# Four staging buffers, an in-place filter product and moved steps in a fused FFT filter, SoLU and maxout kernel

## The chip, the cores and the metric

The kernel runs on one core of a Trainium2 chip. The metric is device time in microseconds (us), the median of three runs. The core has five engines that work side by side, each through its own list of instructions in order: TensorE (PE, matmuls), VectorE (DVE), ScalarE (ACT), GpSimd (POOL) and SyncE (SP, which here only starts DMAs). DMAs started on one engine's list form one queue.

## The reference, cut to what matters

```python
X = np.fft.rfft(x, axis=1)                      # x: (8, 3072, 256), float32
y = np.fft.irfft(X * (filt_r + 1j * filt_i), n=3072, axis=1)
t = y.reshape(8 * 3072, 256)
h = t @ w_in                                    # (256, 1024)
sm = exp(h - h.max(-1)) / (sum + 1e-9)
ln = layer_norm(h * sm) * g_ln                  # over 1024
t = ln @ w_out                                  # (1024, 256)
h = maximum(maximum(t @ w1, t @ w2), t @ w3)    # (256, 768) each
out = h @ w_out2                                # (768, 256)
```

The weights come as 64-bit floats and are turned into 32-bit ones on the chip.

## The kernel before, in words

Every matmul runs on pairs of 16-bit numbers, a high half and a low half of each 32-bit value, in three products. Results lie in PSUM, in a ring of six one-bank tiles (`rtile`, pool `ps_r`) and one two-bank tile for h.

**The FFT.** A sequence of 3072 is taken as 128 x 24. Step a (`a_item`, six pieces) transforms over 128 and stores to a scratch in DRAM (`scr_a`). Step b (`b_item`, u = 0 to 7) loads that back in another layout (`bin`), transforms over 24 and multiplies by the filter: VectorE forms two products p1 and p2 out of PSUM (lines 239, 240), GpSimd adds and subtracts their halves into `yf` (242, 243). Its `late` part splits `yf` into halves `yhl` (ACT 254, DVE 255; for batch 1 the second on GpSimd) and SP transposes them by DMA into `yt` (256). There are two `yhl` tiles, one for each half dc of the channels, used again by every u. Step c (`c_item`) goes back over 24, writes `zo`, transposes it by DMA (279) and stores it (`scr_z`, 291). Step d (`d_item`) loads `din` and goes back over 128. `prep_a` splits the input x for step a: ACT writes `xh` (147), DVE writes `xl` (152). `xh` and `zo` share one tag with two buffers, so an `xh` waits until the `zo` that had its buffer has been transposed away.

**The tiles.** 48 tiles of 512 tokens, six for each of the eight sequences (batches), each go through h (`h_item`, four pieces), z (two), m (six, three banks each: ACT 457 and DVE 459 evacuate, am) and o. The list `ORDER` (line 24; line 23 for the first tile) sets the order of these pieces by letters. The FFT steps of the next batches lie in five slots s0 to s4 of each tile, put there by the `put` calls (lines 702 to 751): for batches from 2 on, b for u = 0 to 7 in slots 0 and 2 of tiles 0 to 3, c for u = 7 in slot 1 of tile 4, and `prep_a` for the batch after that in the same slot behind it.

**The start.** Batch 0 has nothing to hide behind: x, filter and weights are loaded (x and filter on SP's queue, `w_in` on GpSimd's), then come six a pieces, ten rounds of b (round u) and c (round u, piece u-2) with weight work between (`steps`), then d and the first tile, with weight work between its h pieces (`fills`). `get(i)` loads a block of 512 KB of weights, `pre(i)` and `conv(...)` turn it into 32-bit floats (ACT 524, POOL 525; DVE 537, 539, 541).

`run(item)` calls an item's `early` part, then the `late` part that was held from the item before; `flush()` calls the held part at once. An m item's held part goes first.

Of the kernel before, what the change touches and what calls it, by code (L numbers as in the profile page):

```python
# [7 lines left out]
F32 = mybir.dt.float32  # L8
F16 = mybir.dt.float16
# [10 lines left out]
LEAST = 1.125 * 2.0 ** -15  # L20


FIRST = "s0 s1 h2 m0 x0 x1 m1 x0 s2 m2 x0 x0 x0 x0 x2 h3 m3 d m4 m5 g0 f o0 s3 o2 g1 s4"
ORDER = "z0 s0 z1 s1 h2 m0 x0 x0 x1 m1 x0 x0 s2 m2 x2 h3 m3 d m4 m5 g0 f o0 s3 o2 g1 s4"


@with_exitstack
def kernel(
# [41 lines left out]
    mhalf = cst.tile([128, 4], F32, name="mhalf")  # L70
    kap = cst.tile([128, 1], F32, name="kap")
    alpha_w = cst.tile([128, 1], F32, name="alpha_w")
    yhl_t = [cst.tile([128, 8, 128], F16, name=f"yhl{i}") for i in range(2)]

    scr_a = [drm.tile([128, 2, 24, 256], F16, name=f"scr_a{i}") for i in range(2)]
    scr_z = [drm.tile([6, 128, 2048], F16, name=f"scr_z{i}") for i in range(2)]
# [142 lines left out]
    def b_item(b, u):  # L219
        bi, bt, ft = bin_t.pop((b, u)), bt_t.pop((b, u)), f_t.pop((b, u))  # L220
        pss = []
        for dc in range(2):
            ps = rtile("bps")
            for k in range(8):
                o = ps[:, k * 48:(k + 1) * 48]
                xs = bi[:, k, dc * 128:dc * 128 + 128]
                PE.matmul(o, xs, bt[:, k, 0], start=True, stop=False)
                PE.matmul(o, xs, bt[:, k, 1], start=False, stop=True)
            pss.append(ps)
        yfs = []  # L230
        yt = two.tile([128, 2, 8, 128], F16, tag="yt", name="yt")
        yT_t[b, u] = yt

        def early():
            for dc in range(2):
                p1 = two.tile([128, 8, 2, 24], F32, tag="p1", name="p1")
                p2 = two.tile([128, 8, 2, 24], F32, tag="p2", name="p2")
                pv = pss[dc][:, :384].rearrange("p (k r s) -> p k r s", k=8, r=2)
                V.tensor_tensor(p1, pv, ft[:, dc, :, 0:1, :].to_broadcast([128, 8, 2, 24]), op=ALU.mult)
                V.tensor_tensor(p2, pv, ft[:, dc, :, 1:2, :].to_broadcast([128, 8, 2, 24]), op=ALU.mult)  # L240
                yf = two.tile([128, 8, 2, 24], F32, tag="yf", name="yf")
                G.tensor_tensor(yf[:, :, 0, :], p1[:, :, 0, :], p2[:, :, 1, :], op=ALU.subtract)
                G.tensor_tensor(yf[:, :, 1, :], p1[:, :, 1, :], p2[:, :, 0, :], op=ALU.add)
                if u == 0:

                    G.tensor_copy(yf[:, 0, 0, 0:1], p1[:, 0, 0, 0:1])
                    G.tensor_copy(yf[:, 0, 1, 0:1], p2[:, 0, 1, 0:1])
                yfs.append(yf)

        def late():  # L250
            for dc in range(2):
                yv = yfs[dc].rearrange("p k r s -> p k (r s)")
                yhl = yhl_t[dc]
                S.activation(yhl[:, :, 0:48], yv, AF.Copy)
# [447 lines left out]
    for b in range(1, NB):  # L702

        if b == 1:
            for i in range(6):
                put(0, 0, 3 if i < 2 else 4, absmax, 1, i)
            put(0, 0, 4, x_spread, 1)
            put(0, 1, 0, x_scale, 1)
            put(0, 1, 0, prep_a, 1, 0)
            put(0, 1, 0, prep_a, 1, 1)  # L710
            for s in range(6):
                put(0, 1, (1, 1, 2, 3, 3, 4)[s], do_a, 1, s)
            for u in range(2):
                put(0, 1, 2 * u, load_tabs, 1, u)
                put(0, 1, 4, load_b, 1, u)
            put(0, 1, 3, load_c, 1, 0)
        else:
            second = b == 2
            for i in range(6):
                at = ((2, 4), (2, 4), (3, 0), (3, 0), (3, 3), (3, 4)) if second else ((1, 0), (1, 2), (1, 4), (2, 1), (2, 2), (2, 4))  # L720
                put(b - 2, *at[i], absmax, b, i)
            put(b - 2, *((3, 4) if second else (3, 2)), x_spread, b)
            put(b - 2, 4, 0, x_scale, b)

            put(b - 2, 4, 1, prep_a, b, 0)
            put(b - 2, 4, 1, prep_a, b, 1)
            for s in range(6):
                put(b - 2, *((4, 3), (4, 4), (5, 0), (5, 0), (5, 1), (5, 2))[s], do_a, b, s)

            for u in range(2):  # L730
                put(b - 2, 4, 1 + 3 * u, load_tabs, b, u)
                put(b - 2, 5, 2, load_b, b, u)
            put(b - 2, 5, 0, load_c, b, 0)
# [25 lines left out]
    with tc.manual_schedule():  # L759
# [26 lines left out]
        tags = ["din", "din", "z", "ln0", "din", "din", "ln1", "ln2", "z", "ln3", "din", "din", "ln0", "ln1", "u", "u", "yt", "yt", "ao", "ao"]  # L786
        wln.append(two.tile([128, 2, 8, 512], F16, tag="ln", name="wln").rearrange("p a (i c) t -> p (a i) c t", i=2))
        got = {}

# [21 lines left out]
            return job  # L811

        for i in range(4):
            get(i, G)()
        prep_a(0, 0)
        prep_a(0, 1)
        for s in range(6):
            if s == 1:
                load_tabs(0, 0)
                load_tabs(0, 1)  # L820
            do_a(0, s)
            if s < 4:
                size_f(s)
        for s in range(4, 7):
# [9 lines left out]
        for u in range(2):  # L834
# [1 line left out]
        store_rest()  # L836
        load_c(0, 0)
        load_c(0, 1)
        get(6)()
        get(7)()  # L840
        scale_filter()
        scale_f(0, 0)
        scale_f(0, 1)
# [241 lines left out]
```

## Time and profile before

| | |
|---|---|
| median of three runs | 2996.73 us (2991.78 to 2999.52) |
| profiled execution | 2988.05 us, of which the span 2986.3 us |
| busy, share of the span | PE 93%, DVE 68%, ACT 42%, POOL 38% |
| DMA | 368 MB, 762734 packets |

The profile is of one execution, which ran 8.7 us below the median of the three. "Busy" is time in which an engine executed; "idle before" is the time just before an instruction in which its engine had none, with what ended it.

### The profile page before, as it was taken

Reading aid. Unit: us, or ns where it says so; the run is one execution under the profiler, and the core shown is the slowest. Engines: PE = TensorE matmul, PEld = TensorE weight load, DVE = VectorE, ACT = ScalarE, POOL = GpSimd, SP = SyncE. Lnnn points to the kernel's source line nnn. Section 1 sums busy time; section 2 is a strip of 40 time slices with the busy share of each in tenths; the row PEclk is TensorE's granted clock in tenths of the full one; section 3 lists DMA queues with packets and bytes.
Section 4 is the critical chain, followed back from the end, with each engine's and each line's share of the span. In section 5 each row is a group of like instructions: output and inputs, shape, how many; then the busy total and the mean of one; then the engine's idle time right before and its main releaser. Section 6 shows DMA issues by size and latency. Waiting matters only on the chain.

```text
span 2986.3 us, 49502 instructions
## 1 busy us (share of the span) xinstructions
PE 2791.1 (93%) x18992; PEld 1528.4 (51%) x18992; DVE 2016.4 (68%) x3971; ACT 1251.7 (42%) x2058; POOL 1147.5 (38%) x1187
## 2 busy tenths in 40 slices
PE   3478988999999999999999999999999999999999
PEld 1344544555545555455545555555554555555555
DVE  7787666667666776776767677667766767655653
ACT  4444433444344444444444444444444434433332
POOL 4433453245323443343433443234432444323222
PEclk7689999999999999999999999999999999999999
DMA  8924585468445765356733685447644456422221
GB/s 263 237 57 128 151 178 113 119 142 169 100 103 134 152 134 121 109 114 145 166 82 110 130 180 111 95 132 148 142 108 120 114 120 143 100 57 64 50 64 29
DMA packets 762734, 368.35 MB, mean 123 GB/s; under 512 B 650448, under 2 KB 707536, under 8 KB 762496
## 3 DMA queue, kind: packets, MB, share of 16 engines
q1 hardware_dynamic: 732992, 256.21, 39.6%
q0 software_dynamic: 29504, 108.98, 14.0%
q8 instruction: 149, 2.44, 0.4%
q14 instruction: 89, 0.73, 0.1%
HBM read 130.19 MB, written 75.50 MB: 69 GB/s over the span
## 4 chain that ended last, share of the span: by engine, by line
PE 44%; DVE 4%; DMA 3%; issue 2%; ACT 1%; POOL 1%; SPq 0%; ACTq 0%; DVEq 0%; POOLq 0%
PE mps L451 6%; PE mps L452 6%; PE mps L453 6%; PE hps L344 3%; PE hps L346 3%; PE hps L345 3%; PE zps L431 3%; PE zps L432 3%; PE zps L434 3%; PE ops L480 2%; PE ops L479 2%; PE ops L478 2%; DMA yt<-yhl 1%; DVE mx L355 1%; DMA zt<-zo 1%
## 5 line engine op out<-in xcount | busy, mean ns | idle before, releaser
L392 POOL TENSOR_TENSOR ul<-u,uh 128x1024 f16<-128x1024 f32 x191 | 406.5, 2128 | 1172.9 <-issue 627.0
L451 PE MATMUL mps<-z,wm 128*128 128x512 f16 x1728 | 660.2, 382 | 30.1 <-ACT am L457 22.9
L452 PE MATMUL mps<-z,wm 128*128 128x512 f16 x1728 | 659.9, 382 | 0.0
L453 PE MATMUL mps<-z,wm 128*128 128x512 f16 x1728 | 659.3, 382 | 0.0
L459 DVE SCALAR_TENSOR_TENSOR am<-mps,am 128x512 f32<-128x512 f32 x576 | 396.8, 689 | 210.5 <-ACT am L457 138.4
L355 DVE TENSOR_REDUCE mx<-hps 128x1 f32<-128x1024 f32 (+1 forms) x194 | 234.6, 1210 | 224.7 <-PE hps L346 224.4
L361 ACT ACTIVATE u<-hps,mx,scl 128x1024 f32<-128x1024 f32 (+1 forms) x194 | 232.1, 1196 | 357.0 <-DVE mx L358 350.6
L391 ACT ACTIVATE uh<-u 128x1024 f16<-128x1024 f32 x192 | 202.9, 1057 | 354.0 <-DVE u L372 353.9
L463 POOL TENSOR_TENSOR h<-am,h 128x512 f16<-128x512 f32 x240 | 278.4, 1160 | 149.6 <-ACT h L462 149.3
L478 PE MATMUL ops<-wo,h 128*128 128x256 f16 x1152 | 314.0, 273 | 4.2 <-ACT o L484 4.2
L462 ACT ACTIVATE h<-am 128x512 f16<-128x512 f32 x288 | 180.9, 628 | 317.7 <-DVE am L459 317.7
L480 PE MATMUL ops<-wo,h 128*128 128x256 f16 x1152 | 314.0, 273 | 0.0
L479 PE MATMUL ops<-wo,h 128*128 128x256 f16 x1152 | 314.0, 273 | 0.0
L372 DVE SCALAR_TENSOR_TENSOR u<-hps,mx,u 128x1024 f32<-128x1024 f32 (+1 forms) x194 | 246.7, 1273 | 99.0 <-ACT u L361 82.0
L344 PE MATMUL hps<-win,y 128*128 128x512 f16 x768 | 294.0, 383 | 10.8 <-DVE u L372 10.8
L346 PE MATMUL hps<-win,y 128*128 128x512 f16 x768 | 293.3, 382 | 0.8 <-DVE y L320 0.8
L345 PE MATMUL hps<-win,y 128*128 128x512 f16 x768 | 294.0, 383 | 0.0
L452 PEld LDWEIGHTS <-wm 128*128 128x128 f16 x1728 | 169.7, 98 | 233.4 <-issue 43.9
L431 PE MATMUL zps<-ln,wo 128*128 128x512 f16 x752 | 286.6, 381 | 1.8 <-ACT o L484 1.7
L432 PE MATMUL zps<-ln,wo 128*128 128x512 f16 x752 | 286.4, 381 | 0.0
L453 PEld LDWEIGHTS <-wm 128*128 128x128 f16 x1728 | 170.0, 98 | 207.7 <-issue 6.4
L451 PEld LDWEIGHTS <-wm 128*128 128x128 f16 x1728 | 169.9, 98 | 199.0 <-issue 6.2
(191 smaller groups left out, 4448.1 us busy)
## 6 DMA issues: line engine op xcount, KB each, us to landing
out_dram<-o SPq DMA_DIRECT2D x95, 256.0 KB, 2.3
scr_a<-ao SPq DMA_DIRECT2D x47, 512.0 KB, 3.2
scr_z<-zt SPq DMA_DIRECT2D x62, 384.0 KB, 4.4
din<-scr_z POOLq DMA_DIRECT2D x46, 512.0 KB, 5.3
xt<-in_x_dram POOLq DMA_DIRECT2D x42, 512.0 KB, 6.0
ft<-in_filt_dram POOLq DMA_DIRECT2D x56, 384.0 KB, 5.6
bin<-scr_a POOLq DMA_DIRECT2D x56, 384.0 KB, 6.2
bt<-in_dft_b_dram POOLq DMA_DIRECT2D x56, 144.0 KB, 4.0
```

Of the source, the lines that this page charges most:

```text
L344: PE.matmul(o, y[:, dc, 0, tk], win[:, 0, dc, w], start=(dc == 0), stop=False)
L345: PE.matmul(o, y[:, dc, 0, tk], win[:, 1, dc, w], start=False, stop=False)
L346: PE.matmul(o, y[:, dc, 1, tk], win[:, 0, dc, w], start=False, stop=(dc == 1))
L392: (V if (b, g, i) == (0, 0, 3) else G).tensor_tensor(ul, u, uh, op=ALU.subtract)
L431: PE.matmul(ps, wo1[:, 0, c, w], ln[:, 0, c], start=(c == 0), stop=False)
L432: PE.matmul(ps, wo1[:, 1, c, w], ln[:, 0, c], start=False, stop=False)
L451: PE.matmul(pss[k], wm[k][:, 0, dc, w], z[:, dc, 0], start=(dc == 0), stop=False)
L452: PE.matmul(pss[k], wm[k][:, 1, dc, w], z[:, dc, 0], start=False, stop=False)
L453: PE.matmul(pss[k], wm[k][:, 0, dc, w], z[:, dc, 1], start=False, stop=(dc == 1))
L459: V.scalar_tensor_tensor(am, ps, 2.0 ** -15, am, op0=ALU.mult, op1=ALU.max)
L478: PE.matmul(o, h2[:, j, 0, tk], wo2[:, 0, j], start=(j == 0), stop=False)
L479: PE.matmul(o, h2[:, j, 0, tk], wo2[:, 1, j], start=False, stop=False)
```

## The change

1. `yhl_t` has four tiles instead of two; u takes tiles 2 (u mod 2) + dc.
2. GpSimd writes the filter product back into p1 instead of into a tile `yf`. For u = 0 two values are kept in a small tile `mid` first and put back by one copy. So p1 is held until `yhl` has been made of it. In the start a `flush()` is put ahead of rounds 1 and 2.
3. `prep_a` of batches from 2 on goes from slot 1 to slot 2 of tile 4, and in `FIRST` and `ORDER` the whole slot 2 goes behind the third m piece (`s2 m2` becomes `m2 s2`).
4. The four loads of `w_in` go from GpSimd's queue to SP's, behind x and the filter. `get(6)` and `get(7)` go from behind the first c tables into the a pieces; `get(9)` from round 2 to round 0, `get(10)` and `get(11)` from round 4 to 3, `get(12)` and `get(13)` from round 5 to 8, `get(14)` and `get(15)` from round 6 to 9. Their `pre` and `conv` go along: blocks 12 to 15 are converted between the first h pieces instead of ahead of the first d.

```diff
-FIRST = "s0 s1 h2 m0 x0 x1 m1 x0 s2 m2 x0 x0 x0 x0 x2 h3 m3 d m4 m5 g0 f o0 s3 o2 g1 s4"
-ORDER = "z0 s0 z1 s1 h2 m0 x0 x0 x1 m1 x0 x0 s2 m2 x2 h3 m3 d m4 m5 g0 f o0 s3 o2 g1 s4"
+FIRST = "s0 s1 h2 m0 x0 x1 m1 x0 m2 s2 x0 x0 x0 x0 x2 h3 m3 d m4 m5 g0 f o0 s3 o2 g1 s4"
+ORDER = "z0 s0 z1 s1 h2 m0 x0 x0 x1 m1 x0 x0 m2 s2 x2 h3 m3 d m4 m5 g0 f o0 s3 o2 g1 s4"
...
-    yhl_t = [cst.tile([128, 8, 128], F16, name=f"yhl{i}") for i in range(2)]
+    yhl_t = [cst.tile([128, 8, 128], F16, name=f"yhl{i}") for i in range(4)]
...
-                yf = two.tile([128, 8, 2, 24], F32, tag="yf", name="yf")
-                G.tensor_tensor(yf[:, :, 0, :], p1[:, :, 0, :], p2[:, :, 1, :], op=ALU.subtract)
-                G.tensor_tensor(yf[:, :, 1, :], p1[:, :, 1, :], p2[:, :, 0, :], op=ALU.add)
...
+                    t = tiny.tile([128, 2], F32, tag="mid", name="mid")
+                    G.tensor_copy(t[:, 0:1], p1[:, 0, 0, 0:1])
+                    G.tensor_copy(t[:, 1:2], p2[:, 0, 1, 0:1])
+                G.tensor_tensor(p1[:, :, 0, :], p1[:, :, 0, :], p2[:, :, 1, :], op=ALU.subtract)
+                G.tensor_tensor(p1[:, :, 1, :], p1[:, :, 1, :], p2[:, :, 0, :], op=ALU.add)
+                if u == 0:
+                    G.tensor_copy(p1[:, 0, :, 0], t)
...
-            put(b - 2, 4, 1, prep_a, b, 0)
-            put(b - 2, 4, 1, prep_a, b, 1)
+            put(b - 2, 4, 2, prep_a, b, 0)
+            put(b - 2, 4, 2, prep_a, b, 1)
...
         for i in range(4):
-            get(i, G)()
+            get(i)()
...
+            if s in (1, 3):
+                get(6 + s // 2)()
...
+                if u in (1, 2):
+                    flush()
                 run(it)
...
-            [conv(0, 1), get(4), get(5)],
+            [conv(0, 1), get(4), get(5), get(9)],
...
-            [conv(4, 5), split(win[:, :, 0:1], win_32[0], "in"), pre(7)],
-            [split(win[:, :, 1:2], win_32[1], "in"), get(10), get(11), pre(8)],
-            [conv(6, 7), cen[0], pre(9), get(12), get(13)],
-            [cen[1], conv(8, 9), get(14), get(15), pre(10)],
+            [conv(4, 5), split(win[:, :, 0:1], win_32[0], "in"), pre(7), get(10), get(11)],
+            [split(win[:, :, 1:2], win_32[1], "in"), pre(8)],
+            [conv(6, 7), cen[0], pre(9)],
+            [cen[1], conv(8, 9), pre(10)],
...
+            [conv(10, 11), cen[3], cso[0], get(12), get(13)],
...
-            [cs[0][0], pre(16), pre(17)],
-            [conv(16, 17), cs[0][1], cs[1][0], pre(18), pre(19)],
-            [cs[1][1], cs[2][0]],
+            [conv(12, 13), cs[0][0], pre(14), pre(15)],
+            [conv(14, 15), cs[0][1], cs[1][0], pre(16), pre(17)],
+            [conv(16, 17), cs[1][1], cs[2][0], pre(18), pre(19)],
```

ScalarE's list in tile 4 of a batch, from the last c piece to the third h piece, before (`xh` is `prep_a`, `u` the exponentials of h, `am` the evacuation of m, `h_` its high half):

```order
L276 ACTIVATE zo<-cps 128x6x16x4 x2
L147 ACTIVATE xh<-xt,scl 128x1024 x2
L361 ACTIVATE u,st<-hps,mx,scl 128x1024
L457 ACTIVATE am<-mps 128x512
L391 ACTIVATE uh<-u 128x1024
```

and now:

```order
L278 ACTIVATE zo<-cps 128x6x16x4 x2
L363 ACTIVATE u,st<-hps,mx,scl 128x1024
L459 ACTIVATE am<-mps 128x512
L393 ACTIVATE uh<-u 128x1024
L464 ACTIVATE h_4835<-am 128x512
L459 ACTIVATE am<-mps 128x512
L464 ACTIVATE h_4835<-am 128x512
L459 ACTIVATE am<-mps 128x512
L147 ACTIVATE xh<-xt,scl 128x1024 x2
```

The two `xh` stood ahead of h's exponentials and the first m's evacuation; they stand behind the third m's.

VectorE's list in a tile with a b piece in slot 2, before (`p_` are the two products of each half, `am` two instructions for each m):

```order
L459 SCALAR_TENSOR_TENSOR am<-mps,am 128x512 x4
L239 TENSOR_TENSOR p_6099<-bps,ft 128x384
L240 TENSOR_TENSOR p_6100<-bps,ft 128x384
L239 TENSOR_TENSOR p_6106<-bps,ft 128x384
L240 TENSOR_TENSOR p_6107<-bps,ft 128x384
L459 SCALAR_TENSOR_TENSOR am<-mps,am 128x512 x2
L255 TENSOR_TENSOR yhl_88<-yf,yhl_88 128x8x48
L255 TENSOR_TENSOR yhl_89<-yf,yhl_89 128x8x48
L355 TENSOR_REDUCE mx<-hps 128x1
```

and now:

```order
L461 SCALAR_TENSOR_TENSOR am<-mps,am 128x512 x6
L239 TENSOR_TENSOR p_6106<-bps,ft 128x384
L240 TENSOR_TENSOR p_6107<-bps,ft 128x384
L239 TENSOR_TENSOR p_6112<-bps,ft 128x384
L240 TENSOR_TENSOR p_6113<-bps,ft 128x384
L357 TENSOR_REDUCE mx<-hps 128x1
```

The third m's two `am` stand ahead of the four products now, and the two `yhl`, which stood ahead of the fourth h piece's `mx`, stand behind that piece's `u`, ahead of the fourth m's `am`.

SP's list at the end of the c rounds, before (`zt` is the transposed `zo`):

```order
L279 DMA_TRANSPOSE zt<-zo 128x12x128 x2
L288 DMA scr_z_92<-zt 128x2x256 x2
L298 DMA din<-scr_z_92 128x2048 x2
L141 DMA scr_z_92<-zt 128x4x256 x2
L517 DMA wraw<-in_w_dram 128x2x512
```

and now:

```order
L281 DMA_TRANSPOSE zt<-zo 128x12x128
L519 DMA wln<-in_w_dram 128x2x512 x2
L281 DMA_TRANSPOSE zt<-zo 128x12x128
L519 DMA wln<-in_w_dram 128x2x512 x2
L290 DMA scr_z_94<-zt 128x2x256 x2
L300 DMA din<-scr_z_94 128x2048 x2
```

Four weight loads stand between the last transposes and the stores and loads of step d.

## Rows read from the trace of the kernel before

**Rows 1.** Page, part 1: busy time of the engines, share of the span, instructions.
```profile
PE 2791.1 (93%) x18992; PEld 1528.4 (51%) x18992; DVE 2016.4 (68%) x3971; ACT 1251.7 (42%) x2058; POOL 1147.5 (38%) x1187
```
**Rows 2.** Busy time by stretch: length, engines, granted clock, DMA share, GB/s.
```profile
46.00:126.00 80.00, 31.85 (x539) 26.75 (x540) 60.46 (x112) 37.26 (x67) 44.01 (x54) 0.54 1.09 260
138.20:171.70 33.50, 23.73 (x194) 15.41 (x195) 29.56 (x70) 17.01 (x28) 12.91 (x7) 0.89 0.36 103
500.00:2986.30 2486.30, 2441.09 (x16261) 1329.18 (x16259) 1667.68 (x3300) 1041.14 (x1724) 933.88 (x954) 1.00 0.51 115
```
**Rows 3.** PE's waits from 500 us on: releaser, us in total, times, longest.
```profile
PE mps L451 <- ACT am L457: 22.7, 7, 5.4
PE bps L227 <- DVE am L459: 6.0, 6, 1.2
PE aps L161 <- DVE am L459: 5.8, 6, 1.5
```
**Rows 4.** Busy time in five stretches of half clock: the first, and their sum.
```profile
846.40:852.20 5.80, 5.70 (x14) 2.08 (x14) 4.23 (x8) 2.22 (x4) 2.70 (x2) 0.50 0.20 45
...
sum 22.90, PE 18.85 PEld 6.76 DVE 18.71 ACT 10.56 POOL 4.19; mean PE 3.77 PEld 1.35 DVE 3.74 ACT 2.11 POOL 0.84
```
**Rows 5.** Instructions around 840 us: start, us, engine, what, idle before.
```profile
833.58 0.38 PE L451 MATMUL mps<-z,wm 128*128 128x512 f16 x1
840.70 1.15 ACT L147 ACTIVATE xh<-xt,scl 128x1024 f16<-128x1024 f32 x1 [7.68 <-DMA zt<-zo]
846.50 0.59 PE L451 MATMUL mps<-z,wm 128*128 128x512 f16 x1 [4.99 <-ACT am L457]
```
**Rows 6.** VectorE in a tile with b in slot 2, by time.
```profile
732.34 0.55 DVE L239 TENSOR_TENSOR p<-bps,ft 128x384 f32<-128x384 f32 x1
734.20 1.21 DVE L100 TENSOR_REDUCE xm<-xt 128x1 f32<-128x1024 f32 x1
736.72 1.08 DVE L255 TENSOR_TENSOR yhl<-yf,yhl 128x384 f16<-128x384 f32 x2
737.72 1.21 DVE L355 TENSOR_REDUCE mx<-hps 128x1 f32<-128x1024 f32 x1
742.89 1.48 DVE L459 SCALAR_TENSOR_TENSOR am<-mps,am 128x512 f32<-128x512 f32 x2
```
**Rows 7.** Instructions around 412 us, tile 3 of batch 0.
```profile
412.43 0.52 ACT L254 ACTIVATE yhl<-yf 128x384 f16<-128x384 f32 x1 [9.69 <-DMA yt<-yhl]
414.27 0.52 ACT L254 ACTIVATE yhl<-yf 128x384 f16<-128x384 f32 x1 [1.33 <-DMA yt<-yhl]
415.33 0.20 PE L268 MATMUL cps<-ct,yt 96*128 96x48 f16 x1 [9.75 <-ACT am L457]
```
**Rows 8.** VectorE's waits from 0 to 20 us.
```profile
DVE xm L100 <- DMA xt<-in_x_dram: 7.1, 5, 2.7
```
**Rows 9.** First matmul of c for u = 0, 3, 6, and of d.
```profile
61.77 0.22 PE L268 MATMUL cps<-ct,yt 96*128 96x48 f16 x1 [4.03 <-DMA yt<-yhl]
83.94 0.22 PE L268 MATMUL cps<-f,yt 96*128 96x48 f16 x1 [2.81 <-DMA yt<-yhl]
117.29 0.22 PE L268 MATMUL cps<-ct,yt 96*128 96x48 f16 x1 [6.80 <-DMA yt<-yhl]
134.51 0.29 PE L312 MATMUL dps<-dD,din 128*128 128x128 f16 x1 [8.06 <-DMA din<-scr_z]
```
**Rows 10.** ScalarE's waits from 46 to 126 us.
```profile
ACT yhl L254 <- DMA yt<-yhl: 19.7, 9, 5.8
```
**Rows 11.** Conversions on VectorE, and GpSimd beside one of them.
```profile
132.06 0.76 DVE L537 TENSOR_SCALAR wst<-wst 128x512 int32<-128x512 int32 x2
135.14 0.76 DVE L537 TENSOR_SCALAR wst<-wst 128x512 int32<-128x512 int32 x2
150.91 2.11 DVE L537 TENSOR_SCALAR wst<-wst 128x512 int32<-128x512 int32 x2
149.86 2.13 POOL L392 TENSOR_TENSOR ul<-u,uh 128x1024 f16<-128x1024 f32 x1 [0.63 <-ACT uh L391]
```

More of the change, by code (lines that the diff above doesn't have):

```diff
@@ L240, in early @@
                 V.tensor_tensor(p2, pv, ft[:, dc, :, 1:2, :].to_broadcast([128, 8, 2, 24]), op=ALU.mult)
-                yf = two.tile([128, 8, 2, 24], F32, tag="yf", name="yf")
-                G.tensor_tensor(yf[:, :, 0, :], p1[:, :, 0, :], p2[:, :, 1, :], op=ALU.subtract)
-                G.tensor_tensor(yf[:, :, 1, :], p1[:, :, 1, :], p2[:, :, 0, :], op=ALU.add)
                 if u == 0:
-                    G.tensor_copy(yf[:, 0, 0, 0:1], p1[:, 0, 0, 0:1])
-                    G.tensor_copy(yf[:, 0, 1, 0:1], p2[:, 0, 1, 0:1])
-                yfs.append(yf)
+                    t = tiny.tile([128, 2], F32, tag="mid", name="mid")
[5 more added lines that the diff above has]
+                    G.tensor_copy(p1[:, 0, :, 0], t)
+                yfs.append(p1)
         def late():
@@ L252, in late @@
                 yv = yfs[dc].rearrange("p k r s -> p k (r s)")
-                yhl = yhl_t[dc]
+                yhl = yhl_t[2 * (u % 2) + dc]
                 S.activation(yhl[:, :, 0:48], yv, AF.Copy)
@@ L785 @@
             todo += blocks(w_out, wo1_32[i], 4 * i)
-        tags = ["din", "din", "z", "ln0", "din", "din", "ln1", "ln2", "z", "ln3", "din", "din", "ln0", "ln1", "u", "u", "yt", "yt", "ao", "ao"]
+        tags = ["din", "din", "z", "ln0", "din", "din", "ln1", "ln2", "z", "ln3", "din", "din", "ln0", "ln1", "ln2", "ln3", "yt", "yt", "ao", "ao"]
         wln.append(two.tile([128, 2, 8, 512], F16, tag="ln", name="wln").rearrange("p a (i c) t -> p (a i) c t", i=2))
@@ L838 @@
         load_c(0, 1)
-        get(6)()
-        get(7)()
         scale_filter()
@@ L847 @@
         steps = [
-            [conv(0, 1), get(4), get(5)],
+            [conv(0, 1), get(4), get(5), get(9)],
             [conv(2, 3), csw[0], pre(4), pre(5), get(8)],
-            [csw[1], scale("in", 0, 2), pre(6), get(9)],
-            [conv(4, 5), split(win[:, :, 0:1], win_32[0], "in"), pre(7)],
-            [split(win[:, :, 1:2], win_32[1], "in"), get(10), get(11), pre(8)],
-            [conv(6, 7), cen[0], pre(9), get(12), get(13)],
-            [cen[1], conv(8, 9), get(14), get(15), pre(10)],
+            [csw[1], scale("in", 0, 2), pre(6)],
+            [conv(4, 5), split(win[:, :, 0:1], win_32[0], "in"), pre(7), get(10), get(11)],
+            [split(win[:, :, 1:2], win_32[1], "in"), pre(8)],
+            [conv(6, 7), cen[0], pre(9)],
+            [cen[1], conv(8, 9), pre(10)],
             [cen[2], pre(11)],
-            [conv(10, 11), cen[3], cso[0], pre(12), pre(13)],
-            [cso[1], scale("o1", 2, 1), pre(14), pre(15), split(wo1[:, :, 0:4], wo1_32[0], "o1"), split(wo1[:, :, 4:8], wo1_32[1], "o1")],
+            [conv(10, 11), cen[3], cso[0], get(12), get(13)],
+            [cso[1], scale("o1", 2, 1), get(14), get(15), split(wo1[:, :, 0:4], wo1_32[0], "o1"), split(wo1[:, :, 4:8], wo1_32[1], "o1")],
         ]
@@ L904 @@
             V.tensor_tensor(scl[0][:, k:k + 1], scl[0][:, k:k + 1], alpha_w, op=ALU.mult)
-        conv(12, 13)()
-        conv(14, 15)()
+        pre(12)()
+        pre(13)()
         run(d_item(0, 0))
```

## The prediction

> **What bounds the kernel now.** The page's first part comes first: TensorE is busy for 93% of the span, VectorE for 68% [rows 1]. Then the stretches: from 500 us to the end TensorE works 2441.1 of 2486.3 us, so it is the bound there, and what can be won is its 45 us without work and the little that runs at half clock; from 46 to 126 us it works 31.9 of 80 us, at a granted clock of 0.54, while the DMA engines' share is 1.09: the start is bound by transfers and the chain through them [rows 2]. Third, TensorE's waits from 500 us on: 22.7 us in 7 waits of a matmul of m for ScalarE's `am`, 6.0 us of b and 5.8 us of a for VectorE's `am`, six times each [rows 3]. The first of these is one event per batch, and its instructions tell the mechanism: an `xh` of `prep_a` sits on ScalarE with 7.68 us idle before it, until a transpose of `zo` has landed; h's exponentials and the first `am` queue behind it; TensorE, which has filled the six PSUM banks by 841.5, stands for 4.99 us [rows 5]. The same wait, 3.6 to 5.4 us long, comes in five batches; the other two of the 7 are under 0.4 us, so the five hold about 22 us. Towards its end the granted clock falls to half for 3 to 7 us; in those stretches TensorE worked 18.85 us, of which half, 9.4 us, is loss [rows 4].
>
> **The change part by part.** The sum is made against the profiled execution, 2988.05 us, which lies 8.7 us under the median 2996.73; I carry the difference over to the median.
>
> *`prep_a` in slot 2, slot 2 behind the third m.* The `xh` are issued some 11.9 us later: h, then three m of 18 matmuls at 7.93 us for 36 [rows 5]. The third m ends at about 833.6 + 11.9 = 845.5, the transpose had landed by 840.7 [rows 5]: 4.8 us to spare, so the wait should be gone and with it the idle time that precedes the fall of the clock. Gain 22 + 9.4, taken as 31. What is late next is VectorE, which now has the two `xl` between the third m and the fourth h. Before the fourth m's second bank is needed by the fifth m, TensorE has h (12 matmuls, 2.6 us), m (4.0), d (24 of a quarter width, 1.3) and two thirds of an m (2.6): 10.5 us. VectorE's chain in that time: the last `am` 0.7, two `xl` 2.5 (my estimate from the conversion of the same size, `mx`, at 1.21 each), h from `mx` to `am` 742.89 - 737.72 = 5.2, one `am` 0.7 [rows 6]: 9.1 us. It fits. Bounds: gain 20 (a third comes back) to 32.
>
> *b and a behind the third m.* 24 tiles of batches 2 to 7 and 2 of batch 1 have a b in slot 2. The banks that b waited for are free by then, so the 6.0 + 5.8 us [rows 3] go. In return VectorE's four products (734.20 - 732.34 = 1.9 us) and, behind h, the two `yhl` (1.0 us) stand ahead of the fourth m's `am`: 0.7 + 1.9 + 5.2 + 1.0 + 0.7 = 9.5 us against 10.5, and 10.6 in the ten tiles that also take a maximum of x (`xm`, 1.1) there [rows 6]. In the tile of rows 6 VectorE enters the stretch late, and I make it up to 2 us of waiting in about five such tiles, a few tenths in others: 8 to 12 us, against 11.8 saved. Taken as 0; bounds: 12 won to 15 lost.
>
> *Four `yhl`, batch 1.* At 412 us ScalarE stood 9.69 us for the old `yhl` buffer's transpose and held TensorE for 9.75 us [rows 7]. With other buffers the `yhl`, the two `am` behind it and the third m (moved ahead of c) go on: 4 us of work into the gap. c itself needs the very transposes that landed at 412.4 and 414.3 [rows 7], so it cannot start earlier than 412.4, and b comes at about 415; the third m, 4 us, and part of its half clock are saved behind it: taken as 7; bounds 3 to 9.
>
> *The start, x.* VectorE waited 7.1 us in 5 waits for x, 2.7 of them the first transfer's delay [rows 8]; `w_in` shared the DMA engines. Behind x it does not: 4.4 us of waits at most, taken as 3.7. `w_in` itself is first touched 20 us later.
>
> *The start, weight loads.* c went from u = 0 to 3 in 22.2 us and from 3 to 6, the rounds with two loads each, in 33.4 [rows 9]: 3.7 us more for each pair. Two pairs leave these rounds (7.5), two loads leave the time ahead of round 1 for the a pieces (0 to 3.7, taken as 2). But the two pairs stand ahead of the last stores and of `din` on the same queue now, where c's u = 6 to d took 17.2 us [rows 9]: between 0 and 7.5 come back, taken as 4. The trace shows the DMA share at 1.09 in all of that time [rows 2], so work moved inside it costs there what it cost before. The Trainium skill (DMA: Bandwidth & Descriptors, Queues, rings and completion order) says that on each DMA engine the descriptors of one issuing engine's ring are taken in ring order; by that all of the 7.5 us would return and the sum below would be 3.5 us smaller, and no run here shows it yet.
>
> *The start, four `yhl`.* ScalarE waited 19.7 us in 9 waits for the transposes of the round before [rows 10]. With the DMA engines full most of it will be waited elsewhere, by c for `yt`, as it was before each of the rows' c [rows 9]: bounds 0 and 10, taken as 3. The GpSimd work is the same but for one copy more at each u = 0 half; p1 is held longer, but VectorE makes `yhl` itself ahead of the next p1, so nothing new is waited for.
>
> *The start, conversions.* Blocks 12 to 15 were converted from 132.06 on, two pairs at 3.1 us (135.14 - 132.06) [rows 11], while `din` was on its way: d's result had to wait about 1.6 us for them. They go between the h pieces, where VectorE worked 29.6 of 33.5 us [rows 2]: 6.2 us more, less 1.6. Beside GpSimd the first step of a conversion took 2.11 us for two instead of 0.76: a subtraction of GpSimd ran from 149.86 to 151.99 [rows 11]. I take 6.4 us lost; bounds 3 and 9. The Trainium skill (SBUF — State Buffer, Who interferes with whom) has it that VectorE's faster two-port modes and GpSimd exclude each other for a whole instruction, the later one standing until the other ends; the two rows agree, and if every moved first step met a GpSimd instruction the loss would be 6.2 - 1.6 + 2 x 1.35 = 7.3 instead of 6.4.
>
> Start: 3.7 + 7.5 + 2 - 4 + 3 - 6.4 = 5.8 us won; bounds 14 won, 6 lost. All together: 31 + 0 + 7 + 5.8 = 44 us. 2988 - 44 = 2944 for a profiled execution, 2996.7 - 44 = **2953** for the median.
>
> **Rivals.**
> *Half of it.* The five waits go, but slot 2 costs its worse bound (15 lost) and start and batch 1 give nothing: 31 - 15 = 16 us, 2980. For it: the start is bound by DMA, where work is only moved. Against: x and batch 1 show waits that simply lose their cause.
> *The wait comes back.* The `xh` and `xl` stand ahead of the fourth h now; if the chain of 9.1 us is 4 us longer than I add up, the fifth m stands about as long as the third did, and the clock falls again. 44 - 31 = 13 us remain, and with a start that wins nothing 7 us: 2990, no change to tell. Against it: the spare 1.4 us, and ScalarE idle for 7.68 us before.
> *Slower.* The place is the fifth m in the 26 tiles with b in slot 2: VectorE's chain is 9.5 to 10.6 us against 10.5. `yhl` also waits for GpSimd's products, which stand behind the third m's `h`. The cost is 26 us for each microsecond over; it takes more than (44 + 9)/26 = 2.0 us over in each to be slower by over 9 us. At 2.3 us: 44 - 60, so 3013. For it: the chain is within a tenth of the window. Against: only part of the tiles carry the maximum, and VectorE is idle for a third of the span.
> *The ring order of the late loads* by itself moves d by 3.5 us and stays inside the range.
>
> **How the numbers follow.** A measurement of this kernel can tell about 0.3%, 9 us, from no change. Forecast 0.67, half of it 0.15, the wait comes back 0.10, slower 0.08. Faster: 0.67 + 0.15 + a little of the third = 0.83; the same 0.10; slower 0.07. The forecast's own range adds its bounds in part: 31 (20 to 32), slot 2 (15 lost to 12 won), batch 1 (3 to 9), start (6 lost to 14 won); all at their best 67 won, which gives 2930, at their worst 2 won. The range runs from 2930 to 2983, which takes in the second case and leaves the third and fourth out.
>
> **What would show it.** Right: no `xh` with some 7 us idle before it, no matmul of m waiting 3.6 us or more for `am` after 500 us, no half clock after 500 us; the gap of 9.75 us in batch 1 at 3 to 5; VectorE's waits for x at 3 us; d's first matmul between 120 and 130 us. Wrong: waits of m for VectorE's `am` of over 1 us in most tiles with b in slot 2, or d later than 134.5.

## The result, and the profile after

The changed kernel takes **2955.44 us** (median of four runs, 2949.55 to 2963.97) beside 2994.26 us before (2983.62 to 2999.52): ratio 0.9877, 95% interval 0.984 to 0.9914. The profiled execution took 2949.55 us, its span 2947.8, against 2988.05 before: 38.5 us less. Helper lines have moved by two: 451 is 453 now, 457 is 459, 459 is 461, 254 and 255 are 256 and 257, 268 is 270, 312 is 314, 355 is 357, 537 is 539.

Three instants cut the run into parts. The first `mx` of h on VectorE is the end of the FFT start; `amps`, a tiny product that scales the next batch's x, comes once per batch in the tiles, first for batch 1 and then for batch 2. The kernel before, timelines of DVE and PE (start, us, engine, line, operation, tiles, idle before):

```profile
141.33 1.22 DVE L355 TENSOR_REDUCE mx<-hps 128x1 f32<-128x1024 f32 x1 [1.83 <-PE hps L346]
258.32 0.80 PE L116 MATMUL amps<-dg,ones 128*128 128x128 f32 x2 [5.65 <-DVE dg L110]
466.46 0.76 PE L116 MATMUL amps<-dg,ones 128*128 128x128 f32 x2 [1.40 <-DVE dg L110]
```

The changed kernel, the same three rows:

```profile
141.40 1.22 DVE L357 TENSOR_REDUCE mx<-hps 128x1 f32<-128x1024 f32 x1 [1.90 <-PE hps L348]
268.52 0.80 PE L116 MATMUL amps<-dg,ones 128*128 128x128 f32 x2 [5.64 <-DVE dg L110]
467.37 0.77 PE L116 MATMUL amps<-dg,ones 128*128 128x128 f32 x2 [1.51 <-DVE dg L110]
```

So up to the first `mx` nothing is won (0.1 us later); from there to the first `amps` it takes 127.1 us instead of 117.0, **10.1 lost**; between the two `amps` 198.9 instead of 208.1, **9.2 won**; and from there to the end 2480.4 instead of 2519.8, **39.4 won**. The sum is the 38.5 us.

**The tiles.** The changed kernel by stretch (columns as in [rows 2]):

```profile
46.00:126.00 80.00, 31.77 (x539) 26.20 (x536) 62.02 (x116) 35.66 (x63) 42.34 (x54) 0.56 1.04 234
138.20:171.70 33.50, 19.22 (x110) 9.99 (x109) 29.65 (x59) 14.37 (x23) 11.54 (x7) 0.81 0.31 96
500.00:2947.80 2447.80, 2429.49 (x16251) 1325.34 (x16248) 1657.00 (x3299) 1033.41 (x1721) 933.27 (x961) 1.00 0.51 116
```

From 500 us on TensorE is without work for 2447.8 - 2429.5 = 18.3 us; it was 45.2 [rows 2]. Its waits there, changed kernel (releaser, us, times, longest):

```profile
PE mps L453 <- DVE am L461: 9.5, 13, 1.2
PE mps L453 <- ACT am L459: 2.9, 6, 0.5
PE bps L227 <- ACT o L486: 2.2, 1, 2.2
```

The 22.7 us for ScalarE's `am` and the 11.8 us of b and a [rows 3] are gone; m's waits for VectorE's `am`, 4.6 us in nine waits before, are 9.5 now, more than half of them in one tile per batch (below). The half clock after 500 us is one stretch (granted clock third from the end) where [rows 4] had five; it begins when the wait of 2.2 us for ScalarE's `o`, the third row above, ends (651.09):

```profile
651.30:654.70 3.40, 3.40 (x22) 1.44 (x19) 2.08 (x3) 2.81 (x6) 0.00 (x0) 0.50 0.20 77
```

The event of [rows 5], now ScalarE's timeline of the changed kernel in the same tile:

```profile
840.60 0.58 ACT L459 ACTIVATE am<-mps 128x512 f32<-128x512 f32 x1
842.73 0.63 ACT L464 ACTIVATE h<-am 128x512 f16<-128x512 f32 x1 [1.55 <-DVE am L461]
843.26 0.58 ACT L459 ACTIVATE am<-mps 128x512 f32<-128x512 f32 x1
843.74 2.17 ACT L147 ACTIVATE xh<-xt,scl 128x1024 f16<-128x1024 f32 x2
```

The two `xh` follow the third m's `am` without a gap; the 7.68 us in front of them are gone. VectorE's chain behind them held too, though the two `xl` took 3.37 us and not 2.5. The tight place is the tile of [rows 6], with its maximum of x. PE there, changed kernel:

```profile
740.98 0.38 PE L453 MATMUL mps<-z,wm 128*128 128x512 f16 x1 [0.53 <-ACT am L459]
743.61 0.38 PE L453 MATMUL mps<-z,wm 128*128 128x512 f16 x1 [1.17 <-DVE am L461]
```

0.53 + 1.17 = 1.7 us, once in each of five batches.

**Batch 1.** The tile of [rows 7], changed kernel, ScalarE and PE:

```profile
421.11 0.58 ACT L459 ACTIVATE am<-mps 128x512 f32<-128x512 f32 x1
423.01 0.20 PE L270 MATMUL cps<-ct,yt 96*128 96x48 f16 x1 [1.92 <-DMA yt<-yhl]
```

ScalarE evacuates m where it stood 9.69 us for a `yhl` buffer; c waits 1.92 us, not 9.75, and for its own transposes.

**The start.** VectorE's waits for x from 0 to 20 us, changed kernel ([rows 8] had 7.1 us):

```profile
DVE xm L100 <- DMA xt<-in_x_dram: 3.1, 3, 1.5
```

First matmuls of c for u = 0, 3 and 6, and of d, changed kernel (61.77, 83.94, 117.29 and 134.51 in [rows 9]):

```profile
63.96 0.22 PE L270 MATMUL cps<-ct,yt 96*128 96x48 f16 x1 [10.51 <-DMA yt<-yhl]
88.89 0.22 PE L270 MATMUL cps<-f,yt 96*128 96x48 f16 x1 [6.37 <-DMA yt<-yhl]
113.08 0.22 PE L270 MATMUL cps<-ct,yt 96*128 96x48 f16 x1 [5.44 <-DMA yt<-yhl]
135.40 0.29 PE L314 MATMUL dps<-dD,din 128*128 128x128 f16 x1 [12.72 <-DMA din<-scr_z]
```

VectorE waits 4.0 us less for x, and step a's scale, `amps` of batch 0, comes 2.7 us earlier (PE, before and now):

```profile
17.16 0.80 PE L116 MATMUL amps<-dg,ones 128*128 128x128 f32 x2 [17.16 <-DVE dg L110]
14.45 0.79 PE L116 MATMUL amps<-dg,ones 128*128 128x128 f32 x2 [14.45 <-DVE dg L110]
```

By c of u = 0 that is spent: c comes 2.2 us later, with three loads instead of two directly ahead of the first transposes. u = 6 comes 4.2 us earlier, and d, behind the four late loads, 0.9 us later. ScalarE's 19.7 us for the transposes [rows 10] have no row any more in 46 to 126 us, but c's waits for `yt` up to d sum to 34.8 us, against 35.7 before: the wait went elsewhere.

Then the conversions between the h pieces, DVE of the changed kernel:

```profile
145.50 0.75 DVE L539 TENSOR_SCALAR wst<-wst 128x512 int32<-128x512 int32 x2
146.16 1.70 DVE L541 SCALAR_TENSOR_TENSOR wst<-wln,wst 128x512 int32<-128x512 int32 x2
147.78 1.69 DVE L543 SCALAR_TENSOR_TENSOR wst<-wln,wst 128x512 int32<-128x512 int32 x2
149.40 0.68 DVE L357 TENSOR_REDUCE mx<-hps 128x1 f32<-128x512 f32 x1
```

VectorE has no gap here: the second piece's `mx` starts at 149.40, against 145.42 in the kernel before. That pair took 3.9 us. One pair stood ahead of the third piece already in the kernel before; the other new one, between the third and the fourth, took 3.8 us.

### The profile page after: what moved, and what is told of

It is laid out like the page before. It is cut to its first block, busy times and chain, and to the rows that moved or that the text cites. A ratio compares the mean times of both kernels' runs of the same rounds, so it can differ in the third digit from the quotient of the medians.

```text
span 2947.8 us, 49485 instructions
## 1 busy us (share of the span) xinstructions
PE 2780.9 (94%) x18992; PEld 1526.4 (52%) x18992; DVE 2010.1 (68%) x3973; ACT 1245.8 (42%) x2058; POOL 1151.0 (39%) x1199
## 4 chain that ended last, share of the span: by engine, by line
PE 58%; DVE 10%; issue 6%; POOL 3%; ACT 1%; DMA 1%; SPq 0%; DVEq 0%; ACTq 0%; POOLq 0%
PE mps L453 8%; PE mps L454 8%; PE mps L455 8%; PE zps L433 4%; PE zps L434 4%; PE zps L436 4%; PE hps L346 3%; PE hps L347 3%; PE hps L348 3%; PE ops L481 3%; PE ops L482 3%; PE ops L480 3%; DVE am L461 2%; POOL ul L394 1%; DVE mv L378 1%
## 5 line engine op out<-in xcount | busy, mean ns | idle before, releaser
L453 PE MATMUL mps<-z,wm 128*128 128x512 f16 x1728 | 655.7, 379 | 14.8 <-DVE am L461 11.5
```

The source lines that it names most:

```text
L453: PE.matmul(pss[k], wm[k][:, 0, dc, w], z[:, dc, 0], start=(dc == 0), stop=False)
```

## The experiments

Times are medians; ratios are to the kernel before on the same chip, with the 95% interval. The parts of every profile, as cut above (one execution each, us):

| kernel | first mx | mx to amps | amps to amps | to the end |
|---|---|---|---|---|
| before | 141.3 | 117.0 | 208.1 | 2519.8 |
| changed | 141.4 | 127.1 | 198.9 | 2480.4 |
| changed, again (g1) | 143.0 | 127.5 | 202.5 | 2483.3 |
| part 3 alone (e1) | 146.3 | 116.3 | 208.8 | 2485.8 |
| order alone (e2) | 145.4 | 116.3 | 209.4 | 2516.8 |
| prep_a alone (e3) | 145.7 | 116.0 | 208.5 | 2488.7 |
| part 4 undone (e4) | 143.7 | 116.2 | 201.8 | 2484.4 |
| two yhl (f1) | 143.3 | 127.3 | 210.1 | 2482.6 |
| late loads back (f2) | 140.2 | 127.3 | 203.1 | 2483.4 |
| and conversions back (f3) | 145.7 | 116.0 | 202.0 | 2478.8 |
| conversions in rounds (f4) | 144.3 | 118.0 | 202.4 | 2488.9 |
| four blocks less (g2) | 139.3 | 118.0 | 199.1 | 2493.9 |
| f3, w_in on GpSimd (g3) | 145.6 | 117.9 | 202.8 | 2487.9 |
| f3, block 9 later (g4) | 141.0 | 116.2 | 205.9 | 2487.1 |

What is the same code moves by up to 5 us in the first column (before, e1, e2 and e3 have one start), and by some 15 in the last; the second holds to 1 us in these four. A difference of a few us in the first and the last column tells nothing by itself.

**e1, part 3 alone**, on the kernel before:

```diff
-... x1 m1 x0 x0 s2 m2 x2 h3 ...
+... x1 m1 x0 x0 m2 s2 x2 h3 ...
-            put(b - 2, 4, 1, prep_a, b, 0)
+            put(b - 2, 4, 2, prep_a, b, 0)
```

> The kernel before with part 3 alone: slot 2 behind the third m and prep_a in slot 2; buffers, filter product and start as before. My theory (the steady state is won by the move of prep_a, which takes five waits of about 4.5 us and the half clock behind them; b behind the third m gives its 11.8 us of waits back): 31 to 42 us less than before, 2952 to 2963; no matmul of m waits over 3.6 us for am after 500 us, no half clock there but single short ones; the 9.75 us gap of batch 1 stays. Rival (the four yhl buffers and the in-place product are needed for the steady state): under 20 us less. Rival (the chain of VectorE in slot 2 costs): m waits for VectorE's am in most tiles with b, over 5 us in all.

2957.17 us, ratio 0.9869 (0.9848 to 0.9889). Most of the gain is in this part, without any new buffer. m's waits for VectorE's `am` are 11.5 us in 17 waits, 4.6 in nine before: the sum that the second rival named is there, but each wait is 1.2 us at most and the gain stands. Batch 1's gap did not stay as it was: it is 12.82 us, and it is the third m that stands in it, since it now comes ahead of c.

**e2, the order alone** (the first two lines of that diff).

> The kernel before with only the order of slot 2 and the third m exchanged; prep_a stays in slot 1. Theory: the waits of b and a for VectorE's am (6.0 and 5.8 us after 500 us) go, those of m for ScalarE's am behind xh (22.7 us) stay with their half clock: 5 to 12 us less than before. Rival (the exchange itself moves the whole gain, since the third m stands ahead of slot 2 when TensorE is held): over 25 us less, with the five waits gone.

2987.63 us, ratio 0.997 (0.9956 to 0.9984). PE's waits after 500 us:

```profile
PE mps L451 <- ACT am L457: 24.6, 11, 5.4
PE mps L451 <- DVE am L459: 11.2, 15, 1.2
```

and ScalarE's timeline at the event, the `xh` still behind its transpose:

```profile
845.43 1.15 ACT L147 ACTIVATE xh<-xt,scl 128x1024 f16<-128x1024 f32 x1 [7.69 <-DMA zt<-zo]
```

The rival falls: the five waits are all there, and `xh` stands 7.69 us. The waits of b and a went, 11.8 us, and 6.6 us came back in m's waits for VectorE. Timed it wins 9 us (5 to 13); its profile shows 3 of them after the second `amps`. Where the rest is, if it is more than spread, stays open.

**e3, prep_a alone** (the last two lines of that diff and the like for its second half).

> The kernel before with only prep_a moved from slot 1 to slot 2 of tile 4, where slot 2 stands ahead of the third m as before. Theory: the xh are issued h and two m (some 7.9 us) later, at about 841.5 in the event at 840 us, where the transpose they wait for had landed at 840.7: the five waits of over 3.6 us go or shrink under 1 us, 20 to 31 us less than before. The waits of b and a for am stay near 6 us each. Rival (only both moves together are late enough): under 12 us less, xh still idle for some us before the third m.

2960.07 us, ratio 0.9882 (0.9863 to 0.9901). ScalarE at the event:

```profile
840.96 0.59 ACT L457 ACTIVATE am<-mps 128x512 f32<-128x512 f32 x1
845.39 0.58 ACT L457 ACTIVATE am<-mps 128x512 f32<-128x512 f32 x1
845.87 2.17 ACT L147 ACTIVATE xh<-xt,scl 128x1024 f16<-128x1024 f32 x2
```

No idle before `xh`: h and two m are late enough. m waits 1.2 us in all for ScalarE's `am`; a still waits 6.1 and b 4.4 us for VectorE's. This step carries the steady state: 31.1 us in the last column, and timed its ratio stands beside the changed kernel's 0.9877. With the exchange on top (e1) the interval overlaps this one, so the exchange's own worth beside it is not told apart from none.

**f1, two yhl buffers**, on the changed kernel:

```diff
-                yhl = yhl_t[2 * (u % 2) + dc]
+                yhl = yhl_t[dc]
```

> The changed kernel with two yhl buffers instead of four; in-place product and everything else kept. Theory (the four buffers carry the gain in batch 1 and little else): batch 1's gap, 1.92 us in the changed kernel, returns to 10 to 14 us, since the third m stands ahead of slot 2 and so queues behind the same wait; the start's rounds are 0 to 5 us longer; after 500 us no difference. 8 to 16 us more than the changed kernel. Rival (the in-place product, held longer, is what changed batch 1, or c's own transposes bind there anyway): under 5 us more.

2963.26 us, ratio 0.9892 (0.9871 to 0.9912); timed, that overlaps the changed kernel. The trace decides:

```profile
429.15 0.52 ACT L256 ACTIVATE yhl<-p 128x384 f16<-128x384 f32 x1 [14.33 <-DMA yt<-yhl]
430.94 0.59 PE L453 MATMUL mps<-z,wm 128*128 128x512 f16 x1 [11.72 <-ACT am L459]
```

The wait is back with the two buffers, with the in-place product in the kernel. In the third column the five kernels with two buffers mean 209.0, the nine with four 202.1. e4 and e1, which differ only by the four buffers, the in-place product and the two `flush()` calls, have 201.8 and 208.8.

In the start ScalarE's wait for the transposes is back too, 20.7 us from 46 to 126 us, but d's first matmul comes at 136.93, only 0.8 to 1.5 us later than with four (g1 136.18, changed 135.40), which is within the spread of d.

**e4, part 4 undone**, on the changed kernel: `w_in` on GpSimd's queue, all loads, `pre` and conversions where they were.

```diff
-            get(i)()
+            get(i, G)()
...
-            [conv(12, 13), cs[0][0], pre(14), pre(15)],
-            [conv(14, 15), cs[0][1], cs[1][0], pre(16), pre(17)],
+            [cs[0][0], pre(16), pre(17)],
+            [conv(16, 17), cs[0][1], cs[1][0], pre(18), pre(19)],
...
+        conv(12, 13)()
+        conv(14, 15)()
         run(d_item(0, 0))
```

> The changed kernel with part 4 undone: w_in on GpSimd's queue, all weight loads, their pre and conversions at the places they had before; four yhl buffers, in-place product and part 3 kept. Theory (the start of the change lost about 10 us, by the two conversion pairs that stand in VectorE's chain between the h pieces): 6 to 12 us less than the changed kernel, d's first matmul at 130 to 136 us, step a of the next batch (amps) at 255 to 260 us instead of 268.5. Rival (the moved loads and w_in do gain what I predicted, and the later start comes from the four yhl and the in-place product): 4 to 12 us more than the changed kernel, amps at 270 us or later.

2950.80 us, ratio 0.9851 (0.9832 to 0.9871); d at 136.99, `amps` at 259.96. Timed, the kernel is 4.6 us below the changed one's median and 6.8 below g1's, less than the theory's 6 to 12 in one case, and the intervals overlap. The profile decides: `amps` comes 8.6 us before that of the changed kernel and 10.6 before g1's, so part 4 as a whole lost time at the start. Which piece of it, the next two tell. The four buffers and the in-place product are in this kernel, so the rival that blames them falls.

**f2, the four late loads back** in rounds 5 and 6:

```diff
-            [conv(6, 7), cen[0], pre(9)],
-            [cen[1], conv(8, 9), pre(10)],
+            [conv(6, 7), cen[0], pre(9), get(12), get(13)],
+            [cen[1], conv(8, 9), get(14), get(15), pre(10)],
```

> The changed kernel with the loads of blocks 12 to 15 at their old places, rounds 5 and 6 instead of 8 and 9; their conversions stay between the h pieces. Theory A (the conversions in VectorE's chain between the h pieces cost what the start lost): d's first matmul comes 3 to 8 us earlier since din no longer waits behind four loads on its queue, or c's last rounds come later by as much; the stretch from the first mx of h to amps of the next batch stays at 127 us as in the changed kernel (141.40 to 268.5) against 117 in the kernel before. 0 to 5 us less than the changed kernel. Theory B (the loads ahead of din are the loss): d earlier by over 8 us and that shows in full at amps, 8 to 10 us less.

2956.25 us, ratio 0.9873 (0.9855 to 0.9892). d's first matmul:

```profile
133.91 0.29 PE L314 MATMUL dps<-dD,din 128*128 128x128 f16 x1 [7.97 <-DMA din<-scr_z]
```

d waits 7.97 us for `din`, not 12.72, but comes only 1.5 us earlier, since c's last rounds come later by 3.9 (u = 6 at 117.02, not 113.08). The second column stays at 127.3. Theory A.

**f3, their conversions back ahead of d** as well (the last two parts of e4's diff, on f2, with `pre` in rounds 8 and 9).

> The changed kernel with both the loads of blocks 12 to 15 and their conversions at their old places (conversions ahead of d); w_in on SP, the early loads 6, 7 and 9 and the rest kept. Theory A: the stretch from the first mx of h to amps is 117 us again; d's first matmul at 130 to 135; amps at 256 to 261: 7 to 11 us less than the changed kernel, and within 3 us of the kernel with the whole of part 4 undone (the w_in and early loads are worth 0 to 3). Theory B: no difference to the kernel in which only the loads are put back.

**2945.41 us**, ratio 0.9837 (0.9816 to 0.9858), the lowest of all here: f2, on the same chip, took 10.8 us more. The second column falls from 127.3 to 116.0. So the conversions between the h pieces cost 11 us there; ahead of d they cost 2.3 us between d and the first `mx` (8.7 us instead of 6.3). d came at 137.05 and `amps` at 261.68, both a little later than foreseen, so the start kept nothing of the earlier x and loads. One thing of part 4 stays in f2 to g4 that the description of the change does not name: the raw blocks 14 and 15 lie in the buffers `ln2` and `ln3`, no longer in h's `u`.

**f4, a version of my own, conversions in rounds 8 and 9**, on f3: `conv(12, 13)` and `conv(14, 15)` at the end of `steps[8]` and `steps[9]`.

> A version of my own: the changed kernel with the loads of blocks 12 to 15 in rounds 5 and 6 again and their conversions in rounds 8 and 9, beside the transfers of c's last rounds, so that VectorE has none left when din lands. Theory: rounds 8 and 9 wait for transfers, VectorE works 11.9 of 22 us there, so 6.2 us of conversions are hidden and d's result finds VectorE free: 1 to 3 us less than with the conversions ahead of d, 8 to 13 us less than the changed kernel, 2942 to 2947. Rival: the conversions wait for ScalarE's and GpSimd's first steps, and VectorE's halves of c and the last weight split queue behind them: d later by 3 to 8 us and nothing won.

2949.51 us, ratio 0.9849 (0.983 to 0.9867), which overlaps f3. d is not earlier (137.25); the first `mx` follows it in 7.0 us instead of 8.7, but the second column is 118.0. Nothing won: a miss.

**g1, the changed kernel once more.**

> The changed kernel itself once more, beside the next three on one chip, for a second profile of its start: 2950 to 2960; first mx of h at 140 to 144 us, amps of the next batch 126 to 128 us later.

2957.58 us, ratio 0.9884 (0.9865 to 0.9904); the row in the table repeats the 127 us.

**g2, four blocks left out**, on f3; the `get` and `pre` calls of blocks 12 to 15 go as well, so these weights are missing from the result:

```diff
-        conv(12, 13)()
-        conv(14, 15)()
+        for i in range(12, 16):
+            G.memset(todo[i][1], 0.03125)
```

> The version with loads and conversions of blocks 12 to 15 at their old places, but these four blocks (2 MB) are neither loaded nor converted; GpSimd sets their 32-bit weights to a constant. It asks whether a load less shortens the rounds. Theory A (the rounds are bound by the bytes that the DMA engines have to move): 2 MB at the 230 to 270 GB/s that these stretches show are 8 to 9 us; d's first matmul, at 137.05 with the loads, comes 5 to 9 us earlier. Theory B (the rounds are bound by a chain of small transfers, one behind the other, and not by bytes): d within 3 us.

2946.19 us, ratio 0.9846 (0.9831 to 0.9861). d at 132.30, 4.8 us before f3, and 1.6 to 5.0 before f2, f3, f4 and g4, which all have these loads in the rounds: between the two theories. Counted from c of u = 3, which comes at other times in each, d is 4.4 to 4.8 us earlier than in f2, f3, g3 and g4, and 7.0 earlier than in f4: less than the 8 to 9 us of the bytes. The stretch from 46 to 126 us:

```profile
46.00:126.00 80.00, 31.70 (x539) 26.45 (x540) 60.80 (x115) 35.92 (x64) 43.58 (x58) 0.54 1.03 223
```

The DMA share is 1.03 where f3 has 1.06, with 223 GB/s instead of 239. Neither theory is shown; the bytes alone do not set the pace.

**g3, `w_in` on GpSimd's queue**, on f3: `get(i, G)`.

> The version with loads and conversions of blocks 12 to 15 at their old places, and w_in on GpSimd's queue again, beside x. Theory (the 2.7 us that x won are used up before d, since the bytes of w_in move into the time of the a pieces and the first round): amps of batch 0 at 17 us instead of 14.85, d's first matmul and the end within 2 us of the version with w_in on SP. Rival (the x term is real and 2 to 4 us): d and the end 2 to 4 us later.

2954.85 us, ratio 0.9866 (0.985 to 0.9883). `amps` of batch 0 at 17.18 as foreseen, d at 138.25: 1.2 us after f3, 1 to 4.3 after the other three. My theory of nothing left is not upheld and the rival not shown, since the intervals of g3 and g4 overlap; between 0 and 4 us stays open.

**g4, block 9 later**, on f3: `get(9)` from `steps[0]` to `steps[2]`.

> The version with loads and conversions of blocks 12 to 15 at their old places, and the load of block 9 again in round 2 instead of round 0, so that two loads and not three stand ahead of the first transposes on SP. Theory: the first matmul of c at 62 to 63.5 instead of 64.89 us, the wait before it 7 to 9 us instead of 10.36; what is won there is lost again by d: within 3 us at the end. Rival (the chain of transposes from there binds): d 2 us earlier, and 2 us less in all.

2947.65 us, ratio 0.9849 (0.9834 to 0.9864). c's first matmul at 61.72 after a wait of 8.1 us; but f2 and f4, with the third load in place, came at 62.03 and 62.19 too, so that load is not shown to be the delay. d at 134.25; the end is within f3's interval.

## Why the prediction was right, and where it was not

*`prep_a` behind h and the m pieces* (31 foreseen, 20 to 32): right in mechanism, and a little more. e3 alone shows 31.1; the eleven profiles with the exchange too mean 2485.1 in the last column, 34.7 less than before; the pair compared above, 39.4, lies near the favourable end of a spread of 15. The two sources are those named: in that pair TensorE's idle time after 500 us fell by 45.2 - 18.3 = 26.9 us, and TensorE's work at half clock from 18.85 to 3.4, half of the difference being 7.7. The 4.8 us that remain of the 39.4 have no cause shown.

*Slot 2 behind the third m* (0; 12 won to 15 lost): inside. The 11.8 us went, and m's waits for VectorE grew by 9.5 - 4.6 = 4.9. The five tight tiles, where I had put up to 2 us, hold 1.7 each; the rival "slower" needed 2 us over in 26 tiles. I did not see that the exchange puts the third m into batch 1's wait when the buffers stay two (12.82 and 13.85 us in e1 and e2, 9.75 before).

*Four `yhl` in batch 1* (7; 3 to 9): 209.0 - 202.1 = 6.9 by the means, 9.2 in the pair; c's gap is 1.92 us in the changed kernel's first profile and 3.68 in g1, where I had put 3 to 5.

*The start* (5.8 won; 6 lost to 14 won): **this step failed.** At the first `amps` the five profiles with the loads and conversions of the old start (before, e1 to e4) mean 260.9, the three with the new one (changed, g1, f1) 269.9: 9.0 lost, outside my bounds, and 14.8 from what I put. Two parts of it failed.

- **Up to d.** x 3.7 + loads out of rounds 7.5 + loads ahead of the a pieces 2 + `yhl` 3 - late loads 4 = 12.2 won was foreseen. By the same means d came at 136.9 and comes at 136.2: 0.7 won. The means by stretch show where the rest went (us; each stretch begins where the one above it ends; minus is time won; the 3 of the `yhl` belong to no one stretch):

| stretch, up to the first matmul of | old start | new start | change | foreseen |
|---|---|---|---|---|
| `amps` of batch 0 | 17.5 | 14.4 | -3.0 | -3.7 |
| c, u = 0 | 45.7 | 49.6 | +3.9 | -2 |
| c, u = 3 and then u = 6 | 22.3 and 34.0 | 25.3 and 24.3 | +3.0 and -9.7 | -7.5 together |
| d | 17.4 | 22.5 | +5.2 | +4 |

The rounds and the late loads came near what I put. From u = 3 to u = 6 it takes 23.9 to 25.1 us with none of the moved loads there (changed, g1, f1, g2), 30.1 to 31.0 with two pairs (f2 to f4, g3, g4) and 33.4 to 34.7 with three (the old start): about 3 us a pair, where I had 3.7. Most of it came back, between u = 0 and u = 3 and ahead of `din`.

What failed is the credit given ahead of the rounds. x is earlier, but the stretch to the first c became longer by more than that, where I had two loads leave it. Blocks 6 and 7 went into the a pieces, and block 9 came ahead of the first transposes, which I had priced nowhere. The stretch takes 44.6 to 47.1 us in the five profiles with these loads at their old places, e4 with four `yhl` among them, and 47.4 to 50.0 in the nine with 6 and 7 moved, g3 with `w_in` on GpSimd's queue and f1 with two `yhl` among them. So the moved loads go with it, and neither `w_in` nor the buffers; which of the loads, and by what, is not shown. The four `yhl`, 3 foreseen, gave 0.8 to 1.5 us at d (f1), and nothing beside the old loads: e4's 136.99 lies among the 134.5 to 138.5 of the other four.

The Trainium skill (DMA: Bandwidth & Descriptors, Queues, rings and completion order) has descriptors of one ring taken in ring order on each DMA engine. The trace agrees for the late loads: `din`, which needs the last stores of `zt`, is issued 4.1 to 4.2 us after these have been issued in the three profiles with the four loads ahead of the stores, and 1.4 to 1.5 us after them in the eleven without. SP, issue of stores and of `din`, before and then changed:

```profile
127.34 2.16 SPq L288 DMA_DIRECT2D scr_z<-zt  x2
130.91 0.81 SPq L298 DMA_DIRECT2D din<-scr_z  x2
125.74 1.72 SPq L290 DMA_DIRECT2D scr_z<-zt  x2
131.67 0.81 SPq L300 DMA_DIRECT2D din<-scr_z  x2
```

- **The conversions**, 6.4 lost (3 to 9): the stretch from the first `mx` to `amps` is 127.3 instead of 116.4 by these means, 10.9 lost; 1.2 us come back between d and `mx` (1.6 foreseen), so 9.7. From the first to the fourth piece's `mx` the pair of profiles shows 29.1 us against 21.4, 7.7 more: the two new pairs, at 3.9 and 3.8 us instead of the 3.1 that I had taken from rows without GpSimd beside them. The other 2.4 us come behind it. From 178.0 to 186.8 TensorE has z and the next h piece, in 8.8 us at a granted clock of 0.81, where it had been 6.2 us at 1.00 (170.6 to 176.8). About 1.3 us of that is a longer wait of z for a transposed half of `u` (2.02 us instead of 0.71), the rest z's matmuls at half clock between 180 and 184 us. That follow-up I had priced nowhere.

The slow first steps of a pair (`TENSOR_SCALAR`) stand beside GpSimd's `ul` (the low half of `u`), as in [rows 11]; timelines of POOL and DVE, changed kernel:

```profile
153.81 2.14 POOL L394 TENSOR_TENSOR ul<-u,uh 128x1024 f16<-128x1024 f32 x1 [4.00 <-ACT uh L393]
154.86 2.11 DVE L539 TENSOR_SCALAR wst<-wst 128x512 int32<-128x512 int32 x2
164.54 2.12 POOL L394 TENSOR_TENSOR ul<-u,uh 128x1024 f16<-128x1024 f32 x1 [5.02 <-ACT uh L393]
165.79 1.49 DVE L539 TENSOR_SCALAR wst<-wst 128x512 int32<-128x512 int32 x2
```

Of three pairs the first, with no GpSimd instruction beside its first step, took 0.75 there; 2.11 and 1.49 are the two that start within an `ul` (until 155.95 and 166.66). The Trainium skill (SBUF — State Buffer, Who interferes with whom) lets the later of the two stand until the other's instruction ends when VectorE is in a two-port mode. The trace agrees to 0.3 us: the steps are 1.36 and 0.74 us longer, and the `ul` run on for 1.09 and 0.87 us after their start. Of the two new pairs only the third has such a step. The first pair lost its time in the other steps, 1.70 and 1.69 us instead of 1.29 (fence further up); the cause of that is not shown.

So 2953 for 2955.4 is right in its main step and owes its closeness to luck, two misses of opposite sign: the tiles gave more than 31 and the start lost where I had it win. d's first matmul "between 120 and 130 us" was to be the sign of the start, and "later than 134.5" that of being wrong; it came at 135.4. But with the old start it came at 134.5 to 138.5, so the second sign could not tell.

## What to carry to other kernels

When an engine queues for a buffer ahead of work that others need, move the waiting instruction behind that work before adding buffers: here one move of two lines was worth more than all the rest. Loads moved within a stretch that is full of transfers gave little here: three rounds won 9.7 us, and the places that the loads went to lost 8.2. Credit only what leaves such a stretch, and follow every gain to the next wait for a transfer. Do not place filler on an engine that has no gap: here it cost its full length, 7.7 us, and 2.4 us more behind it.

## What the runs showed that I had not expected

Two DMA transposes can hold SP's list for long in the tiles. SP, changed kernel in batch 1 (issue on SP's queue):

```profile
406.49 15.35 SPq L258 DMA_TRANSPOSE yt<-yhl  x2
```

15.35 us for two, 8.60 before around the event of [rows 7], and 1.29 for one of the same size (`uh`) at 418.76 in the kernel before; whatever stands behind them on SP waits. And 2 MB less in the rounds lowered what was moved from 239 to 223 GB/s while the DMA engines' busy share only went from 1.06 to 1.03: a full share here does not mean that time falls with the bytes.
